# A fused attention, expert and gated-MLP kernel: the attention's opening order as a table, and with it the place table, the first gather and the expert row loads

## The chip, the cores and the metric

The kernel runs on one core of a Trainium2 chip. The metric is device time of one execution in microseconds (us), the median of several runs. TensorE (PE) does the matrix products, VectorE (DVE) and ScalarE (ACT) the elementwise work, GpSimd (POOL) some elementwise work and the DMAs with computed row addresses, SyncE (SP) issues most of the other DMAs.

## The reference

```
# 1. decayed linear attention, state per (batch 2, head 8), seq 768, head_dim 48
scale = min(|a|, 0.999) / (|a| + 1e-6); a = (a_re, a_im) * scale       # complex decay per step
S_re, S_im = a * S + (k v^T, 0);   y[t] = q[t] . S_re
# 2. experts: x is y as [1536 tokens, 384]; 8 experts, capacity 384
logits = x @ w_gate; e = argmax(logits); gate_w = softmax(logits)[e]
out[token] = gate_w * relu(row_of_expert @ w1[e]) @ w2[e]              # tokens in order fill an expert's rows
# 3. gated MLP with RMS norm, width 1536
xn = x / sqrt(mean(x^2) + 1e-6) * rms_g
out = (silu(xn @ w_gate) * (xn @ w_val)) @ w_out
```

## The kernel before, in words

**Attention, 0 to 161 us.** The 1536 tokens are 12 chunks of 128 (two batches of six). Two neighbouring chunks are a group; the decay's logarithms and angles are computed for a group at once. For each chunk the prefix sums of the log decays (tile `L`) and of the angles (`TH`, a product with a triangular matrix) give a scaling `R` and a rotation `rot`; keys and queries are scaled (`kqr`), rotated (`K`, `Q`), transposed on PE (`Kp`, `Qp`, copied to `KT`, `QT`), multiplied (`ap`, masked to `AT`), and joined with the carried state (`up`, `z`, `st`) to the output `yp`. The last row of `R` goes through DRAM: SP writes it to `ends`, reads it back as `re` with heads as rows, PE transposes that (`rp`, in `end_decay`), DVE copies it (`rT`), and the state is multiplied with it. `warm` is a matmul without use that runs PE while it has nothing else.

After a chunk comes its routing: `route_1` computes the logits (`xb`, `lg_all`), `choice` the expert (maximum, its index `mi`, as float `mf`, and a row of zeros and a one in `oh_all`), `route_2` and `route_3` count the tokens ahead (`rk`) and give the slot (`slot_all`), and `dispatch` scatters the chunk's rows to `disp` in DRAM, which SP had filled with zeros from the tile `zt` before (`zero`).

**Order.** Each engine's instructions are issued in the order in which the program calls the five `InOrder` wrappers (`ea` ACT, `ev` DVE, `eg` POOL, `et` PE, `sp` SP): what waits on an engine holds up all that is behind it there. The opening, up to the end of chunk 0, is written out by hand (lines 697 to 765); chunks 1 to 11 come from the function `chunk`.

**To the experts.** Expert 0 does not wait for the last two chunks to land in `disp`: their rows are placed by a matmul with a selection matrix `put` (1 where token and slot belong together) into three PSUM tiles `xp_first_at`, `_y`, `_u`, from which ACT and DVE take the high and low parts `hi_first` and `lo_first`.

**Experts, 161 to 311 us.** Eight experts of 8 steps each (n = 0 to 63, 2.1 to 2.3 us each): four steps multiply by a quarter of w1 (`hp`, then `hh`, `hl`), four by a quarter of w2 (`op`). Each weight piece is loaded 8 steps ahead (`raw`) and split into `hi` and `lo` on ACT and DVE 4 steps ahead. `rows_in(e + 1)` loads the next expert's rows (`xd`) at n = 8e, and steps 8e + 4 to 8e + 6 transpose them (`xp`, copied to `xh`, `xl`). Results are written to `ybuf`. Beside this, by the table `more_at`: the **place table**. `meta_steps` computes the softmax weight, the number of tokens per expert (`cnt`, `cnt_sb`, summed up in `cnt_n`), and the place of each token when tokens are sorted by expert; POOL scatters 12 x 128 records of three words (`meta`) to `packed` in DRAM, one at n = 10, 13, ... 43, and SP reads it back as `meta_in` at n = 46. Sorted by expert, the tokens of the first 512-row group of the MLP belong to early experts, so its **gather** (`yt`, four DMAs from `ybuf`) is issued at n = 50, followed by the sums of squares (`jk`), the root (`ms`), the scaling of `yt`, and at n = 61 to 63 its transposes (`mxp`).

**Gated MLP, 311 to 537 us**: three groups of 512 tokens; then the last scatter lands.

Of the kernel before, what the change touches and what calls it, by code (L numbers as in the profile page):

```python
# [17 lines left out]
I32 = mybir.dt.int32  # L18
# [26 lines left out]
def tile_kernel(ctx: ExitStack, tc: tile.TileContext, q, k, v, a_re, a_im, gates, keys, vals, wg, w1, w2, cap, m_gate, m_val, m_out, rms_g, out, dbg=None):  # L45
# [66 lines left out]
    meta_in = const.tile([P, NT, 3], I32, name="meta_in")  # L112
    gw_all = const.tile([P, NT], F32, name="gw_all")
# [10 lines left out]
    packed = dram.tile([N, 3], I32, name="packed")  # L124
# [196 lines left out]
    with ExitStack() as actx:  # L321
# [36 lines left out]

        def tiles(gi):
# [12 lines left out]
        def logs_1(gi, x=ALL):  # L372
            d = gd[gi]
            ea.activation(d["tB"][:, x], d["tA"][:, x], AF.Ln)
            ea.activation(d["tA"][:, x], d["tB"][:, x], AF.Exp, scale=0.5)
            ea.activation(d["l2"][:, x], d["tA"][:, x], AF.Ln, bias=b_eps)

        def logs_2(gi, x=ALL):
            d = gd[gi]
            ev.scalar_tensor_tensor(d["tB"][:, x], d["tB"][:, x], C_MIN, d["tB"][:, x], ALU.min, ALU.add)  # L380
            ev.scalar_tensor_tensor(d["th"][:, x], d["ar"][:, x], 0.0, d["tA"][:, x], ALU.max, ALU.add)
            ev.scalar_tensor_tensor(d["l2"][:, x], d["l2"][:, x], -2.0, d["tB"][:, x], ALU.mult, ALU.add)

        def logs_3(gi, x=ALL):
            d = gd[gi]
            ea.activation(d["th"][:, x], d["th"][:, x], AF.Ln)
            ea.activation(d["th"][:, x], d["th"][:, x], AF.Exp, scale=-1.0)

        def logs_4(gi, x=ALL, e=None):
            d = gd[gi]  # L390
            (e or eg).tensor_tensor(d["th"][:, x], d["ai"][:, x], d["th"][:, x], ALU.mult)
            if 1 < gi < len(groups) - 2:
                load(gi + 2, ["g"])

        def sums(gi, js=range(GM)):
            for j in js:
                c = groups[gi][j]
                L = ps_cs.tile([P, H, D], F32, tag="cs", name=f"L_{c}")
                et.matmul(f2(L), tri, f2(gd[gi]["l2"][:, j]), start=True, stop=True)
                cd[c]["L"] = L  # L400

        def decays(gi, js=range(GM)):
            cs = [groups[gi][j] for j in js]
            for c in cs:
                R = cd[c]["R"] = ch.tile([P, 2, H, D], F32, tag="R", name=f"R_{c}", bufs=4)
                ea.activation(R[:, 0], cd[c]["L"], AF.Exp, scale=-0.5)
                ea.activation(R[:, 1], cd[c]["L"], AF.Exp, scale=0.5)
                sp.dma_start(ends[c:c + 1], R[P - 1:P, 1])
# [8 lines left out]
        def angles_1(gi, x=ALL):  # L417
            ea.activation(gd[gi]["th"][:, x], gd[gi]["th"][:, x], AF.Arctan)

        def angles_2(gi, j):  # L420
            c = groups[gi][j]
# [3 lines left out]
        def turns(gi, j):  # L425

            d, c = gd[gi], groups[gi][j]
# [8 lines left out]
        def angles_3(gi, x=ALL):  # L436
# [3 lines left out]
            ev.tensor_scalar(d["ab"][:, x].bitcast(U32), d["th"][:, x].bitcast(U32), 0x7FFFFFFF, None, ALU.bitwise_and)  # L440

        def angles_4(gi, x=ALL):
# [3 lines left out]
            ea.activation(d["rot"][:, x, :, 1], d["th"][:, x], AF.Sin, scale=-TWO_PI)  # L446
            ea.activation(d["rot"][:, x, :, 0], d["ab"][:, x], AF.Sin, scale=-TWO_PI, bias=b_hpi)

        def scaled(c):

            if c > LAST:
                return
# [3 lines left out]
            ev.tensor_tensor(f4(kq), f4(gd[gi]["kq"][:, j]), f4(d["R"]), ALU.mult)  # L456
            d.update(kr=kq[:, 0], qr=kq[:, 1])
            if j == 1 and gi + 2 < len(groups):
                load(gi + 2, ["kq", "v"] if gi > 0 else ["kq"])

        def frame(c, x, y):

            if c > LAST:
                return
# [4 lines left out]
        def flip(c, hh):  # L469
# [4 lines left out]
            for nm in "KQ":  # L474
# [3 lines left out]
                ea.copy(d[nm + "T"][:, 4 * hh:4 * hh + 4], tp)  # L478
# [11 lines left out]
        def end_decay(c):  # L490
            if c % NC == NC - 1:
                return
# [5 lines left out]
        def state_up(c):  # L498

            d = cd[c]  # L500
            if c % NC == NC - 1:
                return
# [3 lines left out]
            return up  # L506

        def state(c, up=None):
            d = cd[c]
            if c % NC == NC - 1:  # L510
                return
            if up is None:
                up = state_up(c)
# [7 lines left out]
            eg.tensor_tensor(ns[:, :, :D], z, d["rT"][:, :, None].to_broadcast([2 * D, H, D]), ALU.mult)  # L521
            cd[c + 1]["state"] = ns

        def outputs(c):
# [10 lines left out]
            for ps in (slice(0, 2), slice(2, 4)) if c == LAST else (slice(0, 4),):  # L535
                ea.copy(d["yT"][:, ps], yp[:, ps])

        def route_1(i, later=False):
# [8 lines left out]
            (ea.copy if i % 2 == 0 or i > LAST - 3 else ev.tensor_copy)(x_t.rearrange("p (q d) -> p q d", q=4), xb[:, :, :2 * D])  # L547
# [3 lines left out]
            if not later:  # L551
                choice(i)

        def choice(i):
            d, lg = cd[i], lg_all[:, i]
            mx = mx_all[:, i]
            ev.max(mx, lg)
# [4 lines left out]
            ev.tensor_scalar(oh_all[:, i], iota8, mf, None, ALU.is_equal)  # L562
            d["mf"] = mf
            if i > LAST - 2:
                d["mine"] = sm.tile([P, 1], F32, tag="mine", name=f"mine_{i}", bufs=2)
                ev.tensor_scalar(d["mine"], mf, 0.0, None, ALU.is_equal)

        def route_2(i, first=False):
# [6 lines left out]
            if i > LAST - 2:  # L575
                d["put"] = inp.tile([P, GM, 2, H, D], F32, tag="g", name=f"put_{i}").rearrange("p g r h d -> p (g r h d)")[:, :W]
                ev.tensor_scalar(d["put"], iota_w, rk[:, 0:1], d["mine"], ALU.is_equal, ALU.mult)
            d["rk"] = rk
            if not first:
                route_3(i)  # L580

        def route_3(i):
            d = cd[i]
            rk, oh = d["rk"], oh_all[:, i]
# [10 lines left out]

        def dispatch(i):
            eg.indirect_dma_start(disp[:, :], bass.IndirectOffsetOnAxis(ap=slot_all[:, i:i + 1], axis=0), cd[i]["x"][:, :], None)

        LN, TRIG = "natural_log_exp_and_others", "trig_and_small"

        def chunk(c, a, l):

            if c == LAST:
                route_2(c - 1)
                dispatch(c - 1)
            end_decay(c)
            scores(c, 0)
            if c == 1:
                choice(0)
            if l is not None:  # L610
                ea.preload_act_table_set(LN)
                logs_1(l)
            elif a is not None and a > 1:
                ea.preload_act_table_set(TRIG)
                angles_1(a)
            frame(c + 1, "kr", "K2")
            state(c)
            if c + 1 in LOG:
# [575 lines left out]
```

## Time and profile before

| | |
|---|---|
| median of 3 runs | 545.63 us (544.13, 545.63, 547.64) |
| profiled execution | 545.87 us, its span 544.0 us (1.87 us lie around the span) |
| mean granted TensorE clock | 0.986 |
| PE busy | 511.9 us, 94% of the span |
| DVE, ACT, POOL busy | 329.7 us (61%), 292.8 us (54%), 98.6 us (18%) |

The profile is that of one execution. Each row of a timeline is one instruction or a run of equal ones: start and duration in us, engine, operation, tile written <- tiles read; the bracket at its end says how long the engine had been idle before it and what released it. "issue" as releaser means that the profile shows nothing that it waited for. Nearly all instructions carry line 59, that of the `InOrder` helper, so tiles are told by name. The clock is given as a share of TensorE's upper level of 2.4 GHz; 0.50 is its lower level, 1.2 GHz.

### The profile page before, as it was taken

The page shows a single profiled execution, that of the slowest core. Times are in us where ns is not written, and L with a number is a line of the kernel's source. Part 1 is how long each engine was busy: PE and PEld are TensorE (multiplying, and loading weights), DVE is VectorE, ACT ScalarE, POOL GpSimd, SP SyncE. Part 2 cuts the span into 40 slices and gives each one's busy share as a digit, 9 for nine tenths or more (in the row PEclk, how much of TensorE's full clock was granted, in tenths as well). Part 3 has the DMA queues.
Part 4 walks back from the last instruction along what each step waited for, and adds up shares of the span by engine and source line. Part 5 has one row for each costly group of instructions (what it writes and reads, how often), then busy time and mean ns, then how long its engine had stood idle before and what let it go on. Part 6 is the DMA issues. An engine that isn't in the chain of part 4 may idle for free. (4 is left out here: it accounts for less than half of the span.)

```text
span 544.0 us, 8690 instructions
## 1 busy us (share of the span) xinstructions
PE 511.9 (94%) x3298; PEld 451.8 (83%) x3298; DVE 329.7 (61%) x659; ACT 292.8 (54%) x492; POOL 98.6 (18%) x147
## 2 busy tenths in 40 slices
PE   6789998999889999989998899999999999999994
PEld 2467876778789999989998788899988899888894
DVE  4749798797647889888976887751144331333300
ACT  6778697794426776776758465641223421323200
POOL 5022441633710211111030030001400001000011
PEclk9889999999899999999999899999999999999999
DMA  8066714304316999999994262310221100000000
GB/s 302 9 248 214 254 37 151 127 14 161 102 58 231 318 246 292 327 271 312 297 348 138 72 188 87 109 39 30 73 73 29 30 14 31 16 2 0 2 31 33
DMA packets 31419, 72.31 MB, mean 133 GB/s; under 512 B 6877, under 2 KB 13513, under 8 KB 31369
## 3 DMA queue, kind: packets, MB, share of 16 engines
q1 hardware_dynamic: 26505, 61.62, 35.6%
q0 software_dynamic: 2688, 7.10, 3.8%
q10 hardware_dynamic: 2176, 2.95, 1.6%
q8 instruction: 28, 0.46, 0.3%
q14 instruction: 22, 0.18, 0.1%
HBM read 59.67 MB, written 11.98 MB: 132 GB/s over the span
## 5 line engine op out<-in xcount | busy, mean ns | idle before, releaser
L59 DVE TENSOR_TENSOR sg<-vp,sg 128x512 f32<-128x512 f32 x36 | 24.9, 691 | 77.8 <-PE vp L59 75.5
L59 DVE TENSOR_TENSOR lo<-raw,hi 128x768 fp32r<-128x768 f32 x60 | 57.0, 951 | 8.7 <-ACT hi L59 7.9
L59 ACT CAST hi<-raw 128x768 fp32r<-128x768 f32 x64 | 53.2, 834 | 7.5 <-PE op L59 2.8
L59 ACT CAST uh<-sg 128x512 fp32r<-128x512 f32 x36 | 22.3, 621 | 64.6 <-DVE sg L59 62.4
L59 PE MATMUL mop<-oh__3920,uh 128*128 128x384 f32 x144 | 48.7, 338 | 0.0
L59 PE MATMUL mop<-ol__3921,uh 128*128 128x384 f32 x144 | 48.2, 335 | 0.0
L59 PE MATMUL mop<-oh__3920,ul 128*128 128x384 f32 x144 | 48.2, 335 | 0.0
L59 POOL DMA_INDIRECT out<-ot,meta_in x12 | 11.7, 977 | 200.8 <-ACT ot L59 200.8
L59 PE MATMUL op<-hi,hh 128*128 128x384 f32 x128 | 45.9, 359 | 0.0
L59 PE MATMUL op<-hi,hl 128*128 128x384 f32 x128 | 43.9, 343 | 0.2 <-DVE hl L59 0.2
L59 PE MATMUL op<-lo,hh 128*128 128x384 f32 x128 | 43.8, 342 | 0.0
L59 ACT COPY ot<-mop 128x384 f32<-128x384 f32 x12 | 5.7, 479 | 52.8 <-PE mop L59 52.8
L59 DVE TENSOR_TENSOR ul<-sg,uh 128x512 fp32r<-128x512 f32 x36 | 24.8, 688 | 11.9 <-ACT uh L59 11.9
L59 ACT ACTIVATE sg<-gp 128x512 f32<-128x512 f32 x36 | 21.5, 598 | 17.0 <-PE gp L59 16.7
L59 PE MATMUL gp<-mxh,gh 128*128 128x512 f32 x108 | 30.6, 391 | 0.0
L59 PE MATMUL gp<-mxl,gh 128*128 128x512 f32 x108 | 30.4, 389 | 0.0
L59 PE MATMUL gp<-mxh,gl 128*128 128x512 f32 x108 | 30.4, 389 | 0.0
L59 PE MATMUL vp<-mxh,vh 128*128 128x512 f32 x108 | 30.3, 389 | 0.0
L59 PE MATMUL vp<-mxl,vh 128*128 128x512 f32 x108 | 30.3, 389 | 0.0
L59 PE MATMUL vp<-mxh,vl 128*128 128x512 f32 x108 | 30.3, 389 | 0.0
L59 PE MATMUL ap<-QT,KT 96*128 96x128 f32 x192 | 27.4, 287 | 2.4 <-DVE AT L59 1.6
L59 PE MATMUL hp<-xh,hi 128*128 128x240 f32 x168 | 28.4, 276 | 0.8 <-ACT xh L59 0.8
(215 smaller groups left out, 1273.7 us busy)
## 6 DMA issues: line engine op xcount, KB each, us to landing
raw<-in_moe_w SPq DMA_DIRECT2D x64, 384.0 KB
w_g<-in_moe_w_gate SPq DMA_DIRECT2D x9, 512.0 KB
w_v<-in_moe_w_val SPq DMA_DIRECT2D x9, 512.0 KB
w_o<-in_moe_w_out SPq DMA_DIRECT2D x12, 384.0 KB
g<-in_gates SPq DMA_DIRECT2D x5, 768.0 KB
kq<-in_keys SPq DMA_DIRECT2D x5, 768.0 KB
v<-in_vals SPq DMA_DIRECT2D x12, 256.0 KB
disp<-zt SPq DMA_DIRECT2D x4, 768.0 KB
```

The lines of the kernel that those rows point to most:

```text
L59: ins = getattr(self.eng, op)(*args, **kw)
```

## The change

1. **Order.** The hand-written opening and `chunk` are replaced by one string of steps, `ORDER`, and a table `do` that gives the function of each; `'` behind a step puts it on another engine. From chunk 3 on, the order is as before, but for the steps named below. In the opening and chunks 0 to 2 many steps stand elsewhere. `re` of chunk 0 is read right behind its own `ends` write and one zero write, and its transpose stands between the two first `TH` products. The multiplication that ends the angles' logarithms of group 2 (`q.2'`) moves from POOL to DVE, some copies of `QT` and `yT` from ACT to DVE.
2. **The choice.** `oh_all` comes from a TENSOR_TENSOR of `iota8` and the broadcast index, before from a TENSOR_SCALAR. For the last two chunks a new `mine` finds expert 0's tokens as "logit 0 is the maximum", counts them by two small products (`r_10`, `r_11`) and makes `put`; `choice` and `route_2` of the last chunk follow after the copies to `hi_first` and `lo_first`. The three tiles are now one `at` and two `cs`.
3. **The place table** is split over three DRAM tables, each zeroed by a small DMA; `meta_steps` takes two steps per n (n = 1 to 5; before one, n = 1 to 9). All 12 scatters are issued at n = 6, three reads on POOL's queue follow at n = 7, and `join` at n = 30 combines them on DVE by two ORs.
4. **The gather** of the first group moves from n = 50 to n = 41, from the first five experts' part of `ybuf` with a clamped index; the sums of squares to n = 50 to 53, root and scaling to n = 54 and 55. The transposes stay at n = 61 to 63.
5. **The row loads**: `rows_in(e + 2)` is issued at the end of step n = 8e + 6.

```diff
-        u, w = ONE
-        squares(0, u, ev)
...
-        for c in range(1, B * NC):
-            chunk(c, ANG.get(c), LOG.get(c))
...
+        ORDER = """
+            lz.4 sq.0u' sq.0w la.0u lb.0u m0.0u ... R.0 sc.0 ... lc.1 lz.0 n1.0w m2.1 at.0u e.0 q.0w' lg.2 W.27 a.0 at.0w t.0 ab.0u ed.0 a.1 sin.0u L.1 m1.1 K.0 W.6 Q.0 R.1 ...
...
+            rt.10 d.10 s0.11 s1.11 o.11 x.11 fi.0 pi.10 mi.11 pi.11
+        """
+        for line in ORDER.strip().splitlines():
+            for step in line.split():
+                name, at = step.rstrip("'").split(".")
+                do[name](at, step.endswith("'"))
...
-            ev.tensor_scalar(oh_all[:, i], iota8, mf, None, ALU.is_equal)
+            ev.tensor_tensor(oh_all[:, i], iota8, mf.to_broadcast([P, E]), ALU.is_equal)
...
+        def mine(i):
+            lg, mx = lg_all[:, i], mx_all[:, i]
+            ev.max(mx, lg)
+            own = sm.tile([P, 1], BF16, tag="own", name=f"own_{i}", bufs=2)
+            ev.tensor_scalar(own, lg[:, 0:1], mx[:, 0:1], None, ALU.is_ge)
+            r0 = ps_r.tile([P, 1], F32, tag="r", name=f"r0_{i}")
+            et.matmul(r0, ones_b, acc_oh[:, 0:1], start=True, stop=False)
+            et.matmul(r0, strict, own, start=False, stop=True)
...
+            ev.tensor_scalar(put, iota_w, r0, own_f, ALU.is_equal, ALU.mult)
...
+            ea.copy(first[0][:, kk], xps[kk])
+            ev.tensor_tensor(first[1][:, kk], xps[kk], first[0][:, kk], ALU.subtract)
+        choice(LAST)
+        route_2(LAST)
...
-            eg.indirect_dma_start(packed[:, :], bass.IndirectOffsetOnAxis(ap=place[:, i:i + 1], axis=0), meta[:, i], None)
+            eg.indirect_dma_start(packed[i % 3][:, :], bass.IndirectOffsetOnAxis(ap=place[:, i:i + 1], axis=0), meta[:, i], None)
...
-            sp.dma_start(meta_in, packed[0:N, :].rearrange("(t p) c -> p t c", p=P))
+            for j in range(3):
+                eg.dma_start(meta_3[:, j], packed[j][0:N, :].rearrange("(t p) c -> p t c", p=P))
+
+        def join():
+
+            ev.tensor_tensor(meta_in, meta_3[:, 0], meta_3[:, 1], ALU.bitwise_or)
+            ev.tensor_tensor(meta_in, meta_in, meta_3[:, 2], ALU.bitwise_or)
+
+        def first_places():
+
+            ev.tensor_scalar(meta_in[:, :TG, 0], meta_in[:, :TG, 0], (E - 3) * W - 1, None, ALU.min)
+            list(islice(early, TG))
...
-        more_at = {10 + 3 * i: partial(scatter, i) for i in range(NT)}
-        for n in range(1, 9):
-            more_at[n] = partial(next, meta_todo, None)
-        more_at[9] = partial(list, meta_todo)
-        more_at[46] = read_packed
-        for n, steps in ((50, 4), (53, 1), (54, 1), (55, 1), (56, 1), (57, 1), (58, 1), (61, 1), (62, 1), (63, 1)):
+        more_at = {6: lambda: [scatter(i) for i in range(NT)], 7: read_packed}
+        for n in range(1, 6):
+            more_at[n] = lambda: list(islice(meta_todo, 2))
+        more_at[5] = partial(list, meta_todo)
+        more_at[30] = join
+        more_at[41] = first_places
+        for n, steps in ((50, 1), (51, 1), (52, 1), (53, 1), (54, 1), (55, 1), (61, 1), (62, 1), (63, 1)):
...
+        xds = {1: rows_in(1)}
...
-            if more:
-                xd = rows_in(e + 1)
...
+                if j == KD - 1 and e + 2 < E:
+                    xds[e + 2] = rows_in(e + 2)
```

SP's queue from the first `ends` write on, before (`zt` is the tile of zeros; the x behind a row counts equal DMAs):

```order
L59 DMA ends<-R_279 1x384
L59 DMA ends<-R_352 1x384
L59 DMA disp<-zt 512x1x384
L59 DMA re_357<-ends 8x48 x2
L59 DMA re_360<-ends 8x48 x2
```

and with the change:

```order
L59 DMA disp<-zt 128x384
L59 DMA ends<-R_276 1x384
L59 DMA disp<-zt 512x1x384
L59 DMA re_297<-ends 8x48 x2
L59 DMA g_301<-in_gates 128x1536
L59 DMA ends<-R_360 1x384
L59 DMA re_367<-ends 8x48 x2
```

The read of chunk 0's `re` no longer stands behind chunk 1's `ends` write; the zero write of 786 KB still stands ahead of it.

PE around the transpose `rp` of chunk 0, before (`Kp`, `Qp` transposes of `K`, `Q`; `ap` scores; `up` state):

```order
L59 MATMUL L_400<-l_1_273,tri 128x384
L59 MATMUL ap_0_431<-QT_369,KT_370 128x128 x4
L59 MATMUL up_437<-v_214,K_0_335 96x48 x8
L59 MATMUL rp_446<-ident,re_357 96x8
L59 MATMUL ap_1_455<-QT_369,KT_370 128x128 x4
L59 MATMUL yp_461<-AT_430,v_214 64x128 x8
```

and with the change (six `warm` products stand between the last row and `Kp`):

```order
L59 MATMUL warm<-zt,ones_b 128x512
L59 MATMUL TH_330<-th_245,tri_th 128x384
L59 MATMUL rp_338<-ident,re_297 96x8
L59 MATMUL TH_342<-th_245,tri_th 128x384
L59 MATMUL L_347<-l_0_244,tri 128x384
```

`rp` has moved from between chunk 0's products to the front, ahead of the second `TH`.

PE at the turn to the experts, before:

```order
L59 LDWEIGHTS ones_b
L59 MATMUL rk_1943<-acc_oh,ones_b 128x8
L59 LDWEIGHTS strict
L59 MATMUL rk_1943<-oh_all,strict 128x8
L59 MATMUL xp_first_at<-put_1947,x_1919 128x240
L59 MATMUL xp_first_y<-put_1947,x_1919 128x240
L59 MATMUL xp_first_u<-put_1947,x_1919 128x240
L59 MATMUL hp_0_2005<-hi_first,hi_1628 128x240 x3
L59 MATMUL hp_0_2005<-lo_first,hi_1628 128x240 x3
```

and with the change, from the product that follows `own` (waits of the rows in brackets, where DVE or ACT is waited for):

```order
L59 MATMUL r_11_1949<-own_1947,strict 128x1 [waits DVE_49]
L59 MATMUL xp_first_at<-put_1954,x_1930 128x240 [waits DVE_49,Activation_49]
L59 MATMUL xp_first_cs<-put_1954,x_1930 128x240 x2
L59 LDWEIGHTS ones_b
L59 MATMUL rk_1970<-base_b,ones_b 128x8
L59 LDWEIGHTS ones_b
L59 MATMUL rk_1970<-acc_oh,ones_b 128x8
L59 MATMUL hp_0_2021<-hi_first,hi_1634 128x240 [waits DVE_49]
L59 LDWEIGHTS strict
L59 MATMUL rk_1970<-oh_all,strict 128x8 [waits DVE_49]
L59 MATMUL hp_0_2021<-hi_first,hi_1634 128x240 x2
```

`rk` of the last chunk now stands behind the three products into the expert's input, and its last product, which waits for DVE's `oh_all`, inside the first `hp`; the first `hp` now waits for DVE, before for ACT alone.

## Rows read from the trace of the kernel before

**Rows 1.** Windows: length, busy us (and instructions) by engine, clock, DMA share, GB/s.

```profile
20.00:40.00 20.00, 18.08 (x104) 12.51 (x103) 11.83 (x19) 14.60 (x24) 2.78 (x3) 0.83 0.42 154
...
240.00:260.00 20.00, 18.14 (x133) 17.71 (x133) 16.70 (x26) 13.64 (x23) 3.26 (x3) 1.00 1.01 317
...
300.00:320.00 20.00, 18.29 (x86) 16.19 (x87) 16.27 (x33) 11.56 (x20) 3.99 (x4) 0.91 0.36 113
```

**Rows 2.** Timeline of PE in the opening: start, us, instruction, [idle before <-releaser].

```profile
18.99 2.11 PE L59 MATMUL TH<-th,tri_th 128*128 128x384 f32 x4 [2.85 <-ACT th L59]
...
24.66 0.60 PE L59 MATMUL Kp<-ident,K 128*96 128x128 f32 x4
...
32.26 0.18 PE L59 MATMUL rp<-ident,re 8*96 8x8 f32 x1 [1.83 <-DMA re<-ends]
```

**Rows 3.** Timeline of SP's queue in the opening.

```profile
14.56 11.43 SPq L59 DMA_DIRECT2D ends<-R  x2
26.08 0.63 SPq L59 DMA_DIRECT2D disp<-zt  x1
...
26.81 2.45 SPq L59 DMA_DIRECT2D re<-ends  x4
```

**Rows 4.** Timeline of DVE in the opening: the end of chunk 1's queries.

```profile
35.91 0.95 DVE L59 TENSOR_TENSOR Q<-kqr,rot 128x768 f32<-128x768 f32 x1
```

**Rows 5.** Windows of 2 us, behind the wait for `re`.

```profile
34.00:36.00 2.00, 2.00 (x15) 1.39 (x12) 2.00 (x4) 0.52 (x2) 0.01 (x1) 0.50 0.37 152
```

**Rows 6.** Timelines of DVE and POOL: two shapes beside POOL, and `oh_all` without it.

```profile
52.19 1.68 DVE L59 TENSOR_SCALAR oh_all<-iota,mf 128x8 bf16<-128x8 f32 x1
...
135.65 2.58 DVE L59 TENSOR_TENSOR Q<-kqr,rot 128x768 f32<-128x768 f32 x1
...
157.88 0.23 DVE L59 TENSOR_SCALAR oh_all<-iota,mf 128x8 bf16<-128x8 f32 x1
...
52.02 1.82 POOL L59 TENSOR_TENSOR th<-g,th 128x768 f32<-128x768 f32 x1 [4.85 <-ACT th L59]
```

**Rows 7.** Timelines of DVE and PE at the turn to the experts.

```profile
159.78 0.41 DVE L59 TENSOR_SCALAR put<-iota_w,rk,mine 128x240 f32<-128x240 f32 x1 [1.61 <-PE rk L59]
...
162.16 0.41 DVE L59 TENSOR_TENSOR lo_first<-xp_first_u,hi_first 128x240 fp32r<-128x240 f32 x1
...
162.39 0.60 PE L59 MATMUL hp<-lo_first,hi 128*128 128x240 f32 x3
```

**Rows 8.** Timelines of PE and DVE around the count of tokens per expert.

```profile
170.33 0.22 PE L59 MATMUL cnt<-ones_b,acc_oh 128*8 128x128 bf16 x1
...
173.54 0.43 PE L59 MATMUL xp<-ident,xd 128*128 128x128 f32 x2 [0.51 <-DVE cnt_sb L59]
...
173.22 0.27 DVE L59 COPY cnt_sb<-cnt 8x128 f32<-8x128 f32 x1
```

**Rows 9.** Timelines of PE and SP's queue: the rows of an expert that came late.

```profile
242.40 0.30 PE L59 MATMUL xp<-ident,xd 128*128 128x128 f32 x1 [1.64 <-DMA xd<-disp]
...
233.60 2.83 SPq L59 DMA_DIRECT2D xd<-disp  x2
```

**Rows 10.** Timelines of POOL, ACT and PE: the first group's gather and what follows it.

```profile
278.74 1.43 POOL L59 DMA_INDIRECT yt<-ybuf,meta_in  x1 [22.63 <-DMA raw<-in_moe_w]
...
284.38 0.62 ACT L59 ACTIVATE jk<-yt,meta_in 128x384 f32<-128x384 f32 x1 [4.43 <-DMA yt<-ybuf,meta_in]
...
287.54 0.38 PE L59 MATMUL hp<-xh,hi 128*128 128x240 f32 x1 [0.82 <-ACT xh L59]
...
301.70 1.27 PE L59 MATMUL mxp<-ident,yt 128*128 128x128 f32 x4 [3.11 <-issue]
```

**Rows 11.** Timeline of POOL: the scatters to the place table, 12 in all.

```profile
181.84 1.68 POOL L59 DMA_INDIRECT packed<-meta,place  x1 [16.92 <-DVE meta L59]
189.25 1.05 POOL L59 DMA_INDIRECT packed<-meta,place  x1 [5.73 <-DMA packed<-meta,place]
...
208.89 0.97 POOL L59 DMA_INDIRECT packed<-meta,place  x1 [8.06 <-DMA packed<-meta,place]
```

More of the change, by code (lines that the diff above doesn't have):

```diff
@@ L112, in tile_kernel @@
     meta_in = const.tile([P, NT, 3], I32, name="meta_in")
+    meta_3 = const.tile([P, 3, NT, 3], I32, name="meta_3")
     gw_all = const.tile([P, NT], F32, name="gw_all")
@@ L123, in tile_kernel @@
     ybuf = dram.tile([E * W + P, DM], F32, name="ybuf")
-    packed = dram.tile([N, 3], I32, name="packed")
+    packed = [dram.tile([N, 3], I32, name=f"packed_{j}") for j in range(3)]
     ends = dram.tile([B * NC, H, D], F32, name="ends")
@@ L357, in tile_kernel, with act @@
         ONE = [slice(j, j + 1) for j in range(GM)]
+        LN, TRIG = "natural_log_exp_and_others", "trig_and_small"
+        table = [None]
+        def act(need, out, x, func, **kw):
+            if table[0] != need:
+                ea.preload_act_table_set(need)
+                table[0] = need
+            ea.activation(out, x, func, **kw)
         def tiles(gi):
@@ L391, in logs_4, with sums, decays @@
             (e or eg).tensor_tensor(d["th"][:, x], d["ai"][:, x], d["th"][:, x], ALU.mult)
[L392 to L408, printed above, removed]
+        def sums(c):
+            gi, j = group_of[c]
+            L = cd[c]["L"] = ps_cs.tile([P, H, D], F32, tag="cs", name=f"L_{c}")
+            et.matmul(f2(L), tri, f2(gd[gi]["l2"][:, j]), start=True, stop=True)
+        def decays(c):
+            R = cd[c]["R"] = ch.tile([P, 2, H, D], F32, tag="R", name=f"R_{c}", bufs=4)
+            act(LN, R[:, 0], cd[c]["L"], AF.Exp, scale=-0.5)
+            act(LN, R[:, 1], cd[c]["L"], AF.Exp, scale=0.5)
+            sp.dma_start(ends[c:c + 1], R[P - 1:P, 1])
         def ends_in(c):
@@ L477, in flip @@
                     et.transpose(tp[:, h], d[nm + "2"][:, 4 * hh + h].rearrange("p j d -> p (j d)"), ident)
-                ea.copy(d[nm + "T"][:, 4 * hh:4 * hh + 4], tp)
+                (e.tensor_copy if e is not None and nm == "Q" else ea.copy)(d[nm + "T"][:, 4 * hh:4 * hh + 4], tp)
         def scores(c, hh):
@@ L594, in route_3, with first_in @@
             ev.tensor_tensor(acc_oh, acc_oh, oh, ALU.add)
+        first, xps = [], []
+        def first_in():
+            first.extend(wsp.tile([P, KD, W], F32R, tag=tg, name=f"{tg}_first", bufs=LS + 1) for tg in ("hi", "lo"))
+            xps.extend(p.tile([P, W], F32, tag=tg, name=f"xp_first_{tg}") for p, tg in ((ps_at, "at"), (ps_cs, "cs"), (ps_cs, "cs")))
+            for kk in range(KD):
+                for t, n in enumerate((P, REST)):
+                    et.matmul(xps[kk][:, t * P:t * P + n], cd[LAST]["xd"][:n, t, kk * P:(kk + 1) * P], ident[:n, :n], start=t == 0, stop=False)
@@ new lines, in xd_in, with of_group, of_group_on, of_chunk @@
+        def xd_in():
+            xd = cd[LAST]["xd"] = inp.tile([P, GM, 2, H, D], F32, tag="kq", name="xd_first")[:, :, 0].rearrange("p g h d -> p g (h d)")
+            both_halves(xd, 0)
+        def of_group(f, *more, **kw):
+            return lambda at, o: f(int(at[0]), {"u": ONE[0], "w": ONE[1]}.get(at[1:], ALL), *more, **kw)
+        def of_group_on(f, usual, other):
+            return lambda at, o: f(int(at[0]), {"u": ONE[0], "w": ONE[1]}.get(at[1:], ALL), other if o else usual)
+        def of_chunk(f, *more):
+            return lambda at, o: f(int(at), *more)
```

305 lines of the change are left out of this document (87 added, 218 removed).

## The prediction

> **What bounds the kernel now.** I read the windows by stage first. From 320 us to 520 us PE has no gap, so nothing of this change can act there: what it can gain lies before 311 us, where PE is short of its time in single places. The windows that count are those around chunk 0 (PE 18.08 of 20 us busy, clock 0.83), around 240 us (18.14) and at the end of the experts (18.29, clock 0.91) [rows 1]. Then I read PE's timeline for its brackets, the waits in which PE stood, and the timelines of the engine named in each. The reader should see that PE is the engine that sets the time, that its stops are few and short, and that each has another engine's or a DMA's name: the angles' `TH` product waits 2.85 us for ACT, the transpose `rp` 1.83 us for the read of `re` [rows 2]; an `xp` 1.64 us for late rows [rows 9]; `hp` 0.82 us and `mxp` 3.11 us behind the gather [rows 10]. A part of the change is worth at most the stop that it removes, and the half clock that follows some of them.
>
> **The opening.** *The read of `re`.* The read now stands in front of chunk 1's `ends` write, which was issued some 11 us after chunk 0's [rows 3]; so it is early by far more than the 1.83 us that PE stood for it: **-1.8** [rows 2]. *The clock.* Right behind that stop the clock stands at 0.50, which is 1.2 GHz [rows 5]. The window of 20 us has 0.83, that is 0.17 x 20 = 3.4 us of full-speed work lost, in two stretches of about equal length: this one and one behind the `TH` wait [rows 1, 2]. If PE does not stop, up to half of it, 1.7 us, comes back. DVE is not far behind, though: its `Q` of chunk 1, which PE's next transposes need, ends at 36.86 us [rows 4]. I take **-1.0**, between 0 and -1.7. *The transpose at the front.* `rp` now stands between the two `TH` products, and DVE's copy of it ahead of `K`. Before, the zero write was issued at 26.08 us, the reads behind it from 26.81 us, and PE had its `re` at 32.26 us: 6.2 us after the zero write [rows 2, 3]. Now the zero write follows the `ends` write of 14.56 us, so `re` is due at about 15.2 + 6.2 = 21.4 us, where PE could have gone on at some 20.0 us (18.99 and half of the pair's 2.11). Behind `rp` wait the second `TH` product, `L`, six warm-up products and the angles' carry; before `Kp` they took the time from 18.99 us to 24.66 us, much of it at half clock [rows 2]. The warm-ups and DVE's `K` and `Q` cover most of the delay: **+1.0**, between 0 (`re` there in time) and +3 (the read waits for its write to land as well). The wait of `TH` for ACT gets shorter by the reordering, but what it gives goes into this wait; I count nothing for it.
>
> **Chunks 1 and 2.** `oh_all` took 1.68 us in chunk 1, against 0.23 us alone, while POOL multiplied `th` for 1.82 us [rows 6]. That product goes to DVE here, where the same form costs some 0.95 us (the length of DVE's products of 128 x 768, [rows 4]): 1.45 - 0.95 = 0.5 at most, and DVE is not always last: **-0.3**, between -0.5 and 0. In later chunks the product stays on POOL and only the form of `oh_all` changes. The new form reads two tiles of SBUF, and a TENSOR_TENSOR with two such inputs, `Q`, took 2.58 us beside POOL instead of 0.95 [rows 4, 6]: I expect no gain there, 0.
>
> **The turn to the experts.** The two small counting products stand where `rk` stood, and `put` waits for them as before, so the 1.61 us stay [rows 7]. What is new: the first `hp` waits for DVE. Its tile comes to lie on a bank that the expert's input tiles used, so it waits for the last `lo_first`, over at 162.57 us; before, the three products with `hi_first` were done by then and those with `lo_first` began at 162.39 us [rows 7]. That is +0.6. Inside that `hp` stands `rk`'s last product, which waits for the maximum's index, the cast and `oh_all` on DVE, about 0.5 more. `r_10` makes PE wait for `own` once in chunk 11. Saved is the old `rk` ahead of the input, some 0.2. **+1.0**, between 0 and +2.5.
>
> **The place table.** `cnt_n` now follows `cnt` by one step of 2.0 us, before by two. DVE wrote `cnt_sb` 3.2 us after `cnt` had started on PE [rows 8]; so PE stands up to 1.2 us for it, and the old stop of 0.51 us, of a transpose that needed the same PSUM buffer, goes: **+0.5**, between -0.5 and +1.5. Scatters cost POOL 0.97 to 1.68 us of issue each and nothing else, as POOL stood idle for 16.92 us before them [rows 11]. `join` and the clamp put three short instructions on a DVE that is busy 16.70 of 20 us there [rows 1]: **+0.3**, between 0 and 0.6.
>
> **Row loads.** The late rows were issued from 233.60 us and used at 242.40 us [rows 9]. They are now asked for two steps, some 4.4 us, earlier, more than the stop: with its second, shorter half (0.2) **-1.9**, between 0 and -1.9. The DMA engines are full there (1.01 [rows 1]), so other loads become later by the 360 KB / 317 GB/s = 1.1 us of these rows; weight pieces are loaded 8 steps ahead and nothing waits for them in the trace.
>
> **The gather.** ACT stood 4.43 us for `yt`, and behind it lay the copy to `xh` for which PE stood 0.82 us; the rest of the chain (root, scaling) ran so late that `mxp` stood 3.11 us [rows 10]. Issued at n = 41 instead of 50, about 20 us earlier, the rows are there when ACT comes, and the scaling is done at n = 55, six steps ahead of `mxp`: 0.82 + 3.11 = **-3.9**, between -2 (if the scaling on DVE delays `hl` instead) and -4.4. The window 300 to 320 us has a clock of 0.91: 0.09 x 20 = 1.8 us lost, after this stop [rows 1]. With the stop goes the cause: **-1.7**, between 0 and -1.8.
>
> **Sum.** -1.8 - 1.0 + 1.0 - 0.3 + 1.0 + 0.5 + 0.3 - 1.9 - 3.9 - 1.7 = **-7.8 us**, against the profiled execution's 545.87 us (span 544.0 and 1.87 around it): 538.1. That execution lies 0.24 us above the median of the runs, so the forecast is **537.8 us**. With the ends of the terms, not all on one side at once, its own range is 533 to 541.
>
> **Rivals.** *The waits come back (0.18).* In the opening PE then stops at `rp` for as long as it stopped before, and loses the same clock: the terms of the opening and chunk 1 (-2.1) become 0, the turn costs 2 instead of 1, and half of the late clock stays (+0.9): -7.8 + 2.1 + 1.0 + 0.9 = -3.8, 541.8 us. For it speaks that DVE is in order and gets more work in the opening; against it that the two big stops at the experts' end do not depend on it.
>
> *The change does not do what it says (0.09).* The profile names no releaser for the 3.11 us ahead of `mxp` ("issue"). If PE stood there for something other than the scaled `yt`, moving the gather removes only 0.82, and the clock stays low: -7.8 + 3.1 + 1.7 = -3.0, 542.6 us. Against it: the chain ahead of it is ACT's wait for `yt` [rows 10].
>
> *The table's reads on POOL's queue hold up DVE: slower (0.07).* The reads now go out from POOL, each of 1536 pieces of 12 bytes; the trace has only DMAs of 128 pieces on that queue, at 0.97 to 1.68 us of POOL [rows 11]. If this price is one of the DMA, three reads cost 3 us. If it grows with the pieces, it is 12 x 1.0 = 12 us each. The scatters go out at about 174 us; each table's four follow one another at 7.4 us (189.25 - 181.84) to 9.0 us (8.06 + 0.97) [rows 11], so the last lands at about 174 + 4 x 7.4 = 204 us. Reads at 3 x 1 us land by 214 us at the latest, reads at 3 x 12 us at about 245 us. `join` is due at n = 30, at about 228 us. In the second case DVE stands 17 us; PE lives for two steps (4 us) on what is ready, and loses 13 us: 537.8 + 13 = 551 us. It decides from 6.3 us a read on ((228 - 204 - 5) / 3). I take the first price, as the nearest rows, 128 pieces of 12 bytes and 128 of 1536 bytes [rows 10, 11], cost alike. The Trainium skill speaks against this part of the change: in "DMA: Bandwidth & Descriptors", section "SWDGE vs HWDGE vs iDMA", it says that for DMAs issued from GpSimd a program on its cores computes one descriptor pair for each piece moved. By that rule the price would grow with the pieces, and the sum would be that of this rival; no run here shows a DMA of so many pieces on POOL's queue.
>
> **Numbers.** The remaining 0.66 is the forecast. A measurement of this kernel can tell about 1%, 5.5 us, from no change: faster means below 540.2 us. Nine tenths of the forecast lie there (0.59), and a quarter of the two rivals between (0.07): **faster 0.66**. **Slower 0.06** is the last rival but for cases in which the reads cost little over the limit. **Same 0.28** is the rest. The range, **532 to 545**, holds the forecast and the first two rivals; the third is left out, with the far ends of the terms.
>
> **What would show it.** In the opening: `rp` on PE right behind the first `TH`, with a bracket of about 2 us or less, no bracket over 1 us at chunk 0's `ap` or `yp`, and a clock above 0.83 in 20 to 40 us. At the turn: a bracket on the first `hp` with DVE as releaser. In the experts: no bracket at `xp` near 240 us, none at `mxp`, clock 1.00 from 300 to 320 us; POOL's reads from about 204 us, and `join` on DVE without a bracket. The forecast is wrong if PE stands more than 3 us at `rp`, if DVE stands at `join`, or if the stop ahead of `mxp` remains.

## The result, and the profile after

The changed kernel took 539.65 us (median of 20 runs, 536.80 to 542.71), the kernel before 544.07 us (20 runs, 540.59 to 547.64). The ratio is 0.9916, 95% interval 0.9890 to 0.9942: by it the change is 4.6 us (0.84%) faster. Forecast were 7.8 us; the measured time lies in the range. The prediction gave "faster" 0.66 and "same" 0.28 and drew the line between them at about 1%; the measured gain is real, but lies on the side of "same".

Profiled execution: 540.29 us, span 538.6 us. The page's head, and the windows that answer to [rows 1], with 180 to 240 us added:

```profile
span 538.6 us, 8714 instructions
...
PE 505.4 (94%) x3301; PEld 447.3 (83%) x3302; DVE 333.3 (62%) x669; ACT 289.8 (54%) x488; POOL 100.2 (19%) x149
```

```profile
20.00:40.00 20.00, 18.94 (x131) 14.20 (x131) 16.28 (x27) 14.88 (x24) 3.14 (x4) 0.96 0.56 195
...
180.00:240.00 60.00, 55.49 (x400) 53.52 (x400) 50.35 (x81) 39.15 (x69) 12.01 (x11) 1.00 0.97 277
240.00:260.00 20.00, 20.00 (x153) 19.93 (x153) 18.45 (x31) 15.21 (x27) 0.00 (x0) 1.00 1.00 338
...
300.00:320.00 20.00, 20.00 (x100) 17.40 (x99) 16.38 (x31) 12.52 (x23) 4.78 (x4) 1.00 0.50 149
```

In this execution the stops of the opening, of the late rows near 240 us and of the experts' end are gone, as forecast. New is a loss of 4.5 us between 180 and 240 us, where PE had been without a gap before:

```profile
180.00:240.00 60.00, 60.00 (x451) 59.81 (x450) 55.74 (x92) 43.94 (x78) 11.01 (x9) 1.00 0.96 291
```

PE's timeline in the opening, for [rows 2]:

```profile
17.90 1.34 PE L59 MATMUL TH<-th,tri_th 128*128 128x384 f32 x2 [1.91 <-ACT th L59]
19.18 0.24 PE L59 MATMUL rp<-ident,re 8*96 8x8 f32 x1
19.35 1.65 PE L59 MATMUL TH<-th,tri_th 128*128 128x384 f32 x2
...
23.81 0.60 PE L59 MATMUL Kp<-ident,K 128*96 128x128 f32 x4
...
32.02 0.66 PE L59 MATMUL yp<-AT,v 128*64 128x128 f32 x8 [0.56 <-DVE AT L59]
```

`rp` stands at the front without a bracket: `re` was there. The 1.83 us are gone, and no bracket above 0.6 us took their place in chunk 0 of this trace (six other traces of the new order have one of 0.70 to 0.95 us at `L`, near 25 us).

PE at the turn to the experts and at the count, for [rows 7, 8]:

```profile
146.50 0.16 PE L59 MATMUL r<-own,strict 128*128 128x1 bf16 x1 [0.73 <-DVE own L59]
...
156.59 0.64 PE L59 MATMUL xp_first_at<-put,x 128*128 128x240 f32 x2 [0.61 <-DVE put L59]
...
158.93 0.38 PE L59 MATMUL hp<-hi_first,hi 128*128 128x240 f32 x1 [0.86 <-DVE lo_first L59]
159.46 0.17 PE L59 MATMUL rk<-oh_all,strict 128*128 128x8 bf16 x1 [0.16 <-DVE oh_all L59]
...
167.38 0.38 PE L59 MATMUL cnt_n<-tri,cnt_sb 8*128 8x7 f32 x2 [1.36 <-DVE cnt_sb L59]
```

Four new waits for DVE (`own`, `lo_first`, `oh_all`, `cnt_sb`), each where the prediction put it. The wait for `put` is still there (0.51 us before).

PE, then ACT, in the new loss between 180 and 240 us:

```profile
188.23 0.32 PE L59 MATMUL xp<-ident,xd 112*128 112x112 f32 x1 [0.79 <-DMA xd<-disp]
...
213.88 0.43 PE L59 MATMUL xp<-ident,xd 128*128 128x128 f32 x2 [1.92 <-DVE xl L59]
...
232.18 0.43 PE L59 MATMUL xp<-ident,xd 128*128 128x128 f32 x2 [0.90 <-DVE xl L59]
```

```profile
189.19 0.84 ACT L59 CAST hi<-raw 128x768 fp32r<-128x768 f32 x1 [2.83 <-DMA raw<-in_moe_w]
...
205.16 0.33 ACTq L59 DMA_DIRECT2D ybuf<-yd  x1
205.53 0.57 ACT L59 ACTIVATE hh<-hp 128x480 fp32r<-128x480 f32 x1 [1.11 <-DMA raw<-in_moe_w]
```

ACT waits for weight pieces, 6.8 us in all, which it did not do in this window before. The row of `hh` has to be read with care. `hh` uses `hp` and not the piece; on ACT's queue it stands right behind the second `ybuf` write of an expert's results, and the wait lies ahead of that write. The profile puts its end down to the landing of a `raw` load; why the write waits for one, its views do not show. `hh` comes late, DVE's `hl` and `xl` behind it, and PE stops for `xl`.

POOL, DVE and PE from the place table to the gather, for [rows 10, 11]:

```profile
206.04 0.97 POOL L59 DMA_INDIRECT packed<-meta,place  x1 [4.71 <-DMA packed<-meta,place]
207.01 2.16 POOL L59 DMA_DIRECT2D meta<-packed  x2
212.35 1.22 POOL L59 DMA_DIRECT2D meta<-packed  x1 [3.18 <-DMA packed<-meta,place]
...
264.72 1.07 POOL L59 DMA_INDIRECT yt<-ybuf,meta_in  x1 [51.15 <-PE xp L59]
```

```profile
235.75 0.19 DVE L59 TENSOR_TENSOR meta_in<-meta 128x36 int32<-128x36 int32 x1
```

```profile
276.01 0.61 ACT L59 ACTIVATE jk<-yt,meta_in 128x384 f32<-128x384 f32 x1
```

```profile
298.44 0.60 PE L59 MATMUL mxp<-ident,yt 128*128 128x128 f32 x4
```

`join`, the sums of squares and `mxp` run without a wait for what they use. The third read stood 3.18 us for a scatter, with nothing behind it on POOL until the gather.

### The profile page after: what moved, and what is told of

It reads as the page before. It is cut to its first block, busy times and chain, and to the rows that moved or that the text cites. A ratio compares the mean times of both kernels' runs of the same rounds, so it can differ in the third digit from the quotient of the medians.

```text
span 538.6 us, 8714 instructions
## 1 busy us (share of the span) xinstructions
PE 505.4 (94%) x3301; PEld 447.3 (83%) x3302; DVE 333.3 (62%) x669; ACT 289.8 (54%) x488; POOL 100.2 (19%) x149
## 5 line engine op out<-in xcount | busy, mean ns | idle before, releaser
L59 POOL DMA_INDIRECT yt<-ybuf,meta_in x12 | 13.5, 1127 | 93.6 <-PE xp L59 51.2
```

The source lines that it names most:

```text
L59: ins = getattr(self.eng, op)(*args, **kw)
```

## The experiments

Three questions: does the new loss hang on the row loads, on the table's burst of scatters, or on chance; what each part of the change is worth; and whether the stops of the trace before stand in every execution. Ratios are to the kernel before, run beside each.

**A ledger by PE's marks**, which every experiment uses. Each column is the time on PE from the first start of one tile to the next, in us, so that a row adds up to the span: start to `up` of chunk 0; OPENING to `xb` of chunk 3; CHUNKS to `xb` of chunk 10; TURN to the first `hp`; COUNT to `op` of n = 6; MIDDLE to `op` of n = 44; GATHER to the first `gp`; the rest.

| kernel | start | OPENING | CHUNKS | TURN | COUNT | MIDDLE | GATHER | rest | span |
|---|---|---|---|---|---|---|---|---|---|
| before | 28.95 | 42.85 | 77.27 | 12.32 | 15.15 | 83.63 | 51.37 | 232.50 | 544.03 |
| r2_before_again | 28.86 | 42.83 | 77.78 | 12.32 | 15.15 | 81.35 | 53.28 | 232.28 | 543.85 |
| change | 28.42 | 40.06 | 76.25 | 14.20 | 15.70 | 87.47 | 44.08 | 232.39 | 538.56 |
| r1_change_again | 27.52 | 40.06 | 77.68 | 14.21 | 15.70 | 82.98 | 44.02 | 232.56 | 534.73 |
| e1_old_row_loads | 27.93 | 40.05 | 76.23 | 14.20 | 15.71 | 83.98 | 44.00 | 232.49 | 534.59 |
| e2_old_table | 28.76 | 40.05 | 76.24 | 14.21 | 14.89 | 81.50 | 51.38 | 231.91 | 538.95 |
| e3_old_experts | 27.49 | 40.05 | 76.24 | 14.20 | 14.90 | 81.36 | 50.88 | 232.32 | 537.44 |
| d4_old_attention | 27.69 | 42.69 | 77.80 | 12.32 | 15.94 | 83.34 | 45.32 | 232.40 | 537.51 |
| e5_old_turn | 28.31 | 40.06 | 76.28 | 12.25 | 15.95 | 83.31 | 44.62 | 232.11 | 532.89 |
| e6_count_later | 28.17 | 40.07 | 77.71 | 14.21 | 14.22 | 83.18 | 44.34 | 232.23 | 534.12 |
| e8_order_alone | 28.32 | 40.04 | 77.46 | 12.25 | 15.14 | 82.00 | 50.47 | 232.62 | 538.30 |
| e9_scatters_spread | 27.99 | 40.06 | 76.25 | 14.20 | 15.71 | 84.49 | 44.18 | 232.62 | 535.50 |
| e10_steps_late | 28.23 | 40.06 | 77.25 | 14.20 | 14.89 | 84.21 | 44.16 | 232.76 | 535.76 |
| e7_combined | 27.79 | 40.05 | 77.57 | 12.25 | 14.48 | 82.33 | 43.99 | 232.33 | 530.79 |

OPENING, TURN and COUNT agree within 0.2 us wherever the code there is the same, so one trace is enough for them. COUNT also depends on the turn before it: with the old turn it is 0.25 us longer, with the old table (15.15 for 14.89) as with the new one (15.95 for 15.70). CHUNKS is 76.2 to 76.3 us where the half-clock stretch near 137 us is missing, and 77.3 to 77.8 us where it is there: in all three traces of the old order and in five of eleven of the new. MIDDLE varies by up to 4.5 us between traces of one kernel, so a difference there needs several.

**The change again** (no edit):

> The changed kernel once more, unaltered, for a second trace and as the base of this set. Three theories of the experts' new stops (PE lost 5.0 us between 188 and 232 us in the first trace, at six transposes of the rows). LOADS: the DMA engines are full, the row loads asked for two steps earlier push the weight pieces back; the stops stand at the same places again, 3 to 6 us in all. BURST: the 12 scatters at n = 6 and the three reads of 1536 pieces slow the engines between 174 and 219 us; same places again. CHANCE: the full engines lose some us in every execution, at places that vary; then the sum or the places differ by over 2 us here. Time 0.991 of the kernel before in all three.

537.53 us (12 runs), ratio 0.9905 (0.9873 to 0.9936). MIDDLE is 82.98, in the first trace 87.47. Of the six stops two remain, 0.35 us at 209.92 and 0.88 us at 228.23 us: 1.2 us in all, for 4.4 us in the first trace. A difference of over 2 us is the sign of CHANCE; the next runs ask whether chance is all.

**The row loads put back:**

```diff
-        xds = {1: rows_in(1)}
...
+            if more:
+                xd = rows_in(e + 1)
...
```

> The change with its row loads put back to n = 8e. LOADS: the stops between 188 and 232 us are gone (under 1 us in all), the one near 240 us for late rows is back with about 2 us; some 2 to 3 us faster than the change. BURST: the stops between 188 and 232 us stay (4 to 5 us) and the one near 240 us comes on top; some 2 us slower than the change. CHANCE: 2 to 5 us of stops somewhere between 180 and 260 us, time within 1 us of the change.

536.18 us (6 runs), ratio 0.9880 (0.9831 to 0.9929), not to be told from the change. ACT's waits for weight pieces remain (3.6 us between 180 and 240 us), MIDDLE is 83.98: the row loads are not their cause. PE's stops between 188 and 232 us are 1.7 us, which is over the 1 us of the theory LOADS and below the 2 us of CHANCE and the 4 us of BURST. The stop near 240 us did not come back either.

**The old table and gather**, row loads early:

```diff
-        more_at = {6: lambda: [scatter(i) for i in range(NT)], 7: read_packed}
+        more_at = {10 + 3 * i: partial(scatter, i) for i in range(NT)}
...
-        more_at[41] = first_places
...
```

> The change with the place table and the first gather as before (one table, a scatter every third step from n = 10, one read by SP at n = 46, gather at n = 50), row loads early. All theories: the stops at hp (0.8 us) and mxp (3.1 us) near 286 and 298 us and the half clock behind return, +5.8 and +1.5 us, and cnt_n's wait of 1.4 us goes. LOADS: the stops between 188 and 232 us stay, 4 to 5 us; the time is 5 to 6 us above the change. BURST: they go (under 1 us); the time is within 2 us of the change. CHANCE: 2 to 5 us of them, somewhere.

540.79 us (12 runs), ratio 0.9965 (0.9935 to 0.9995). GATHER is back at 51.38, and MIDDLE falls to 81.50: no wait of ACT for weight pieces, PE without a gap:

```profile
180.00:240.00 60.00, 60.00 (x449) 59.58 (x449) 56.02 (x89) 45.27 (x79) 10.94 (x10) 1.00 0.97 299
```

The time, 3.3 us above the change, lies between the two forecasts; the stops are gone, as BURST has it. The waits go with the new table, not with the row loads.

**The attention alone** (the two edits above together: table, gather and row loads old):

> The new order of the attention and the new choice alone; place table, gather and row loads as before. All theories: about 2.5 us ahead of the kernel before at the first hp, as in the change's trace. LOADS and BURST: from there as before, no stops between 188 and 232 us, the late rows near 240 us cost 2 us, gather stops return: 2.5 to 3 us faster than before, ratio about 0.995. CHANCE: stops of 2 to 5 us between 180 and 260 us here too, since the experts start earlier and the loads do not; ratio 0.995 to 1.0.

541.68 us (11 runs; a twelfth took 549.11), ratio 0.9993 (0.9960 to 1.0026). No stops in MIDDLE (81.36), and none for late rows, with the old row loads. The profiled execution, 539.18 us, was the fastest of the runs.

**The kernel before, again** (no edit):

> The kernel before, unaltered, for a second trace. Theory STEADY: the stops of the first trace on which the prediction rests (rp 1.8 us, late rows 1.6 us near 240 us, mxp 3.1 us) and its half-clock stretches at 33, 139 and 303 us stand at the same places. Theory CHANCE: the stops that hang on the order (rp, mxp) are there, the late rows and single half-clock stretches are not, or elsewhere; first hp then at 158.5 to 161.4 us (161.39 in the first trace).

543.89 us (8 runs), ratio 0.9997. On the stops CHANCE holds: `rp` and the gather's are there (`mxp` with 2.0 us), the late rows are not. On the clock STEADY does: the half-clock stretches stand at the same places (32.5, 138.3, 302.2 us), with a fourth at 288.5 us. The first `hp`, at 161.79 us, lies outside the window that CHANCE gave. The only bracket of its PE between 230 and 280 us:

```profile
263.40 0.43 PE L59 MATMUL xp<-ident,xd 128*128 128x128 f32 x2 [0.42 <-DVE xl L59]
```

**The attention as before** (the kernel before, with table, gather and row loads new):

> Attention, choice and turn as before; place table, gather and row loads new. If the new order of the attention is worth the 3.4 us that the traces show at chunk 4, less the 2 us that the turn to the experts costs: ratio 0.993 to 0.995, some 1.5 to 2 us above the change. If the attention's part is worth nothing, as the run of it alone suggests (0.9993), 0.990 to 0.991 like the change. In the trace: rp's stop of 1.8 us there, mxp's gone, cnt_n's of 1.4 us there.

538.29 us (6 runs), ratio 0.9900 (0.9865 to 0.9936), as the change. The trace shows why: OPENING loses 2.6 us against the change, TURN gains 1.9 us, and COUNT loses 0.25 us.

**The old turn to the experts:**

```diff
-            ... x.10 mi.10 ch.10 f1.11 d.9 xd.0
+            ... x.10 ch.10 f1.11 d.9 xd.0
-            rt.10 d.10 s0.11 s1.11 o.11 x.11 fi.0 pi.10 mi.11 pi.11
+            rt.10 d.10 s0.11 s1.11 o.11 x.11 ch.11 fi.0 pi.10 rf.11 pi.11
```

(`rf` is the first half of the old `route_2`; `put` and `route_3` as before.)

> The change with the old way through the last two chunks: choice and rk before put, the three input tiles in at, y, u. Theory TURN (the first hp waits for DVE, own and oh_all hold PE): PE gains 0.7 at r_10, 0.9 and 0.2 at the first hp, first hp 6.0 to 6.5 us behind the chunk's xb instead of 6.7, in all 1.5 to 2 us faster than the change, ratio 0.987 to 0.988. Rival: the old chain (index, cast, oh_all, rk, put) takes as long, no difference.

534.85 us (6 runs), ratio 0.9847 (0.9814 to 0.9880). The column TURN is 12.25 for 14.20, 1.95 us, as the theory has it; 0.25 us of that comes back in COUNT. The ratio falls by more than this (0.6%, some 3 us). The new turn is a loss:

```profile
155.76 0.67 PE L59 MATMUL xp_first_at<-put,x 128*128 128x240 f32 x2 [0.51 <-DVE put L59]
...
156.90 1.16 PE L59 MATMUL hp<-hi_first,hi 128*128 128x240 f32 x3
```

**The count one step later:**

```diff
-        for n in range(1, 6):
-            more_at[n] = lambda: list(islice(meta_todo, 2))
+        for n, cnt in ((1, 2), (2, 2), (3, 1), (4, 2)):
+            more_at[n] = lambda cnt=cnt: list(islice(meta_todo, cnt))
```

> The change with cnt_n two steps behind cnt, as before, place table otherwise new. Theory: PE's stop of 1.4 us at cnt_n goes and nothing takes its place; 1.4 us faster, ratio 0.988 to 0.989. Rival: the stop only moves (0.5 us at a transpose, as before, and the rest lost again where the loads are the limit): within 0.5 us of the change.

534.81 us (6 runs), ratio 0.9823 (0.9794 to 0.9851). COUNT is 14.22 for 15.70, 1.48 us, and `cnt_n` has no bracket:

```profile
169.21 0.38 PE L59 MATMUL cnt_n<-tri,cnt_sb 8*128 8x7 f32 x2
```

The ratio falls by more (0.8%, 4.5 us) than this stop; the trace, of the slowest of the six runs, does not show the rest.

**The order alone** (the edits of e3_old_experts and e5_old_turn together):

> The new order of the opening and of chunks 0 to 2 (with the new form of oh_all) alone; the turn to the experts, place table, gather and row loads as before. Theory ORDER: from chunk 0's up to chunk 4 the order gains 2.8 us in every trace so far and nothing takes it back once the turn is the old one: 2.8 to 3.5 us faster than before, ratio 0.9935 to 0.995; no half-clock stretch near 33 us. Rival LATER: what the opening gains comes back at the stops behind it (late rows, hp and mxp behind the gather): ratio 0.998 to 1.000, as the order with the new turn gave (0.9993).

539.95 us (12 runs), ratio 0.9957 (0.9930 to 0.9984), 2.3 us faster; OPENING gains 2.8 us, TURN and COUNT are as before. That is nearer to ORDER, with a little less than forecast; the end of the interval touches LATER.

**Scatters spread:**

```diff
-        more_at = {6: lambda: [scatter(i) for i in range(NT)], 7: read_packed}
+        more_at = {6 + 2 * i: partial(scatter, i) for i in range(NT)}
+        more_at[29] = read_packed
...
```

> The change with its 12 scatters one at a time, at n = 6, 8, ... 28, the three reads at n = 29 and join at n = 37; meta_steps as early as in the change. ACT waited 2.3 to 6.8 us for weight pieces between 180 and 240 us in the six traces with the new table, not at all in the four with the old one. BURST (the scatters close together slow the loads): these waits go, or drop below 1 us, and PE's stops between 188 and 215 us with them; 1.5 to 2.5 us faster than the change, ratio 0.986 to 0.988. EARLY (the steps of the place table at n = 1 to 5 hold DVE, the pieces are asked for later and stay late): waits of 2 us and more remain, ratio as the change, 0.990 to 0.991.

539.16 us (12 runs), ratio 0.9919 (0.9887 to 0.9951). ACT still waits 5.1 us for weight pieces, MIDDLE is 84.49. But the edit did not spread the scatters. It moved them in the program, and POOL, which had nothing else to do between them, issued them as before: from 173.1 to 199.8 us, with the reads from 202.1 us (in the change from 173.6 to 206.0 us, reads from 207.0 us).

```profile
173.13 1.74 POOL L59 DMA_INDIRECT packed<-meta,place  x1 [11.49 <-DVE meta L59]
...
199.78 0.97 POOL L59 DMA_INDIRECT packed<-meta,place  x1 [0.30 <-issue]
202.06 1.10 POOL L59 DMA_DIRECT2D meta<-packed  x1 [1.32 <-DMA packed<-meta,place]
```

So BURST is not tested by this run. But for the later `join` it is in effect a third run of the change.

**Table steps late:**

```diff
-        more_at = {6: lambda: [scatter(i) for i in range(NT)], 7: read_packed}
-        for n in range(1, 6):
-            more_at[n] = lambda: list(islice(meta_todo, 2))
+        more_at = {10: lambda: [scatter(i) for i in range(NT)], 11: read_packed}
+        for n in range(1, 9):
+            more_at[n] = partial(next, meta_todo, None)
...
```

> The change with the place table's steps at the old pace (one at n = 1 to 8, the rest at n = 9), then all 12 scatters at n = 10, the reads at n = 11, join at n = 37. EARLY (two steps of the table per n at the start hold DVE, weight pieces are asked for later and stay late): ACT's waits for weight pieces between 180 and 240 us fall below 1 us, PE's stops there below 1 us, and cnt_n's 1.4 us become 0.5: 2.5 to 3 us faster than the change, ratio 0.985 to 0.987. Rival TABLE (three tables and their three reads from POOL's queue slow the loads, whenever the steps run): waits of 2 us and more and PE's stops of 1.5 us and more remain; only cnt_n's stop gets shorter, ratio 0.988 to 0.990.

537.05 us (6 runs), ratio 0.9889 (0.9851 to 0.9926). ACT waits 3.3 us, and the chain to PE is the same as in the change:

```profile
220.21 0.33 ACTq L59 DMA_DIRECT2D ybuf<-yd  x1
220.58 0.57 ACT L59 ACTIVATE hh<-hp 128x480 fp32r<-128x480 f32 x1 [2.25 <-DMA raw<-in_moe_w]
```

```profile
228.93 0.43 PE L59 MATMUL xp<-ident,xd 128*128 128x128 f32 x2 [2.29 <-DVE xl L59]
```

EARLY falls as well; the ratio is the one that TABLE expected. With the count later the waits did move: ahead of 199 us there are none here and in e6_count_later and 0.3 us in e7_combined, for 1.2 to 5.2 us in the six traces with the change's early count. But MIDDLE is no shorter for it (84.21 us here, 83.18 in e6_count_later, 82.98 in the second trace of the change).

**Combined** (the edits of e1_old_row_loads, e5_old_turn and e6_count_later together):

> The change with what the runs so far speak for: the old way through the last two chunks, cnt_n two steps behind cnt, row loads at n = 8e. Theory ADD: the gains of the three add up (2 us of the turn, 1.5 of the count, about 1 of the row loads): 4 to 5 us faster than the change, ratio 0.979 to 0.983. Rival LIMIT: from 180 us on the full DMA engines set the time, what comes earlier waits there for weight pieces: ratio 0.984 to 0.987, and PE's stops between 188 and 232 us grow beyond 3 us.

531.59 us (6 runs), ratio 0.9792 (0.9755 to 0.9830). ADD holds: 11.3 us ahead of the kernel before and 6 us ahead of the change, the fastest version of this study. As a ledger the three fit better: TURN and COUNT gain 3.2 us on the change. ACT's waits for weight pieces are 0.9 us here, and PE is short of 0.8 us:

```profile
180.00:240.00 60.00, 59.20 (x438) 58.73 (x438) 55.72 (x90) 44.53 (x78) 12.43 (x11) 1.00 0.98 306
```

**What stays open.** ACT waited for weight pieces between 180 and 240 us in all nine traces with the new table (0.9 to 6.8 us). In the five with the old one it waited 0.8 us once, and in r2_before_again 2.05 us just behind that window (at 244.06 us). The row loads are not the cause, and the early count decides where ACT waits, more than how long MIDDLE is. The cause is not shown. The three reads on POOL's queue cannot be all of it: in the change, every wait but 0.26 us ended before the first read was issued (207.01 us). The burst of scatters is an untested rival. With one table each scatter waited for the one before it to land, and the twelve took from 181.8 to 255.1 us; with three tables they took from 173.6 to 206.0 us. Against it stands that their own transfers filled 0.8% of the DMA engines' time between 173 and 207 us. No run spread the scatters, and none took away the three reads or the table's three parts alone.

## Why the prediction was right, and where not

The direction was right and the range held; the size was nearly twice the measured one. That the range held owes something to luck: it is 13 us wide, and errors of both signs, most of them of 0.7 to 1.9 us, cancelled in part. By the prediction's own steps:

- **Opening, chunks 1 and 2: -2.1 forecast, -2.8 measured** (OPENING 42.84 to 40.06, in each of eleven traces). `rp`'s stop went; the half-clock stretch behind it, at 33 us in the three traces with the old order, is in none with the new one. The +1.0 for `rp` at the front did not come: `re` landed by 19.2 us and not at 21.4 us. The step failed in taking the old landing, 6.2 us behind the zero write, as the price; here it took at most 4.5 us from the zero write at 14.70 us (4.2 us in the second trace, where `rp` stood 0.23 us for it). Why it was quicker is not shown.
- **`oh_all`: -0.3 forecast.** In chunk 1 it took 0.17 us, but what followed on DVE was held up in its place, as POOL now squared `sq` there (55.65 to 57.45 us); PE stood 1.04 us behind it:

```profile
55.65 1.80 POOL L59 TENSOR_TENSOR sq<-sq 128x768 f32<-128x768 f32 x1
...
56.03 1.45 DVE L59 SCALAR_TENSOR_TENSOR slot_all<-slf_all,over,spare 128x1 int32<-128x1 f32 x1
```

```profile
58.73 0.91 PE L59 MATMUL TH<-th,sel 128*128 128x384 f32 x2 [1.04 <-DVE th L59]
```

  This stop of 1.04 us stands in all eleven traces of the new order, so the term came out as a loss; the -2.8 above holds it. In the later chunks beside POOL the new form bought nothing, as argued; for [rows 6]:

```profile
71.22 1.71 DVE L59 TENSOR_TENSOR oh_all<-iota,mf 128x8 bf16<-128x8 f32 x1
```

- **Turn: +1.0 forecast, +1.9 measured.** The three waits were named rightly. `lo_first` cost 0.86 us for 0.6, `oh_all` 0.16 for 0.5, and `own`, which had no price of its own in the sum, 0.73 us. DVE's stop ahead of `put` stayed, as read (1.61 us before, 1.79 after). COUNT gives 0.25 us of the loss back.
- **Place table: +0.5 for the count, +0.8 measured.** COUNT rose by 0.55 us, but the new turn lowers it by 0.25 us; at the same turn the new table costs 0.8 us (15.70 for 14.89, 15.95 for 15.15). `join` ran without a wait; its +0.3 shows in no row.
- **Row loads: -1.9 forecast, 0 measured.** This step failed. The late rows near 240 us stood in the trace that the prediction read, but not in the second trace of the same kernel, not in e3_old_experts with the same row loads, and with 0.43 us in e8_order_alone. It priced one execution's chance.
- **"Weight pieces are loaded 8 steps ahead and nothing waits for them": failed.** With the new table ACT waits for them, and MIDDLE takes 82.3 to 87.5 us for 81.4 to 83.6. That is the cover that went: +1.6 us between the second traces of both kernels, +3.8 us between the first. Why they come late stays open (above); the prediction had priced the new table by its stops at `cnt_n` and `join` alone.
- **Gather and its clock: -5.6 forecast, -7.3 measured** (GATHER 51.37 to 44.08). Up to the first `mxp` it is 5.2 us (3.9 forecast): `hp`'s and `mxp`'s stops went, and with them a third one of 0.25 us. Behind it, it is 2.1 us (1.7 forecast): gone is the half-clock stretch near 300 us, which stands in all five traces with the old gather and in none of the nine with the new one.

The ledger's sum, with COUNT's net 0.55: -2.8 + 1.9 + 0.55 + 1.6 - 7.3 = -6.05 us, and with the first trace's MIDDLE (+3.8) -3.85 us; measured were -4.6 us. It leaves out the start and CHUNKS, which vary by 1 to 1.5 us between traces of one kernel. The forecast's other error was its base: 545.63 us was the median of three runs, 544.07 us that of twenty.

**The rivals.** "The waits come back" came nearest in size, -3.8 us, and its turn of 2 us came true; but the rest was lost at another place, in the middle of the experts and not in the opening. "The change does not do what it says" fell: `mxp` stood for the scaled `yt`. The slower one fell by its price: a read of 1536 pieces cost POOL 1.05 to 1.22 us in the change's two traces, no more than a scatter of 128 (0.97 to 1.74 us). The Trainium skill ("DMA: Bandwidth & Descriptors", section "SWDGE vs HWDGE vs iDMA") has GpSimd compute a descriptor pair for each piece; the POOL rows show no growth of the issue with the pieces, 128 to 1536.

## What to carry to other kernels

Before a stop of the trace is priced, ask whether the code makes it (an order, a wait that is queued behind something) or the load of the DMA engines in that execution. The columns OPENING, TURN and COUNT, of the first kind, agreed to 0.2 us between traces of the same code; MIDDLE, of the second, came and went by 4 us. A change of several parts should be priced and tried by parts; here two of them (the turn, the early count) cost 3.2 us of what the others gained, and without them and with the old row loads the ratio is 0.979 instead of 0.991. The waits for DVE at the seam of two stages (0.73, 0.86 and 0.16 us) came out in TURN as 1.9 us: nothing there covered them. And the scatters, moved in the program, were not moved on the chip, as POOL had nothing to do in between: the trace of a run shows whether its edit did what it was meant to do.

## What the runs showed of the hardware

- The same stop of 1.76 us (`Qp` waiting for `Q`, in all fourteen traces, over at 133.9 to 138.3 us) goes with a stretch at 1.2 GHz in eight of them, begun between 0.3 us before its end and 1.0 us after, and with none in six; with the stretch CHUNKS is 1.0 to 1.6 us longer.
- On DVE an instruction on a single column ([128 x 1], 0.22 us) took 1.45 us beside a POOL product of 1.80 us: an instruction so small was held up until the product was over (57.48 and 57.45 us).
